# Sliding-window attention into a hard-swish feed-forward: first-tile stores moved to the Pool queue, opening loads, casts and matmuls re-ordered

## The chip, the cores and the metric

The kernel runs on one core of a Trainium2 chip. The metric is device time of one execution in microseconds (us). Eight runs of the kernel before gave a median of 342.49 us (341.08 to 343.52). The profile is one further look at a single execution, the one that took 342.05 us.

## The reference

Inputs are float32: q, k, v of 8 batches x 8 heads x 576 tokens x 64, and two weights, w_in (512 x 2048) and w_out (2048 x 512). The output is 4608 tokens x 512 in float32.

```python
scores = q @ k.T / sqrt(64)
mask = (rel >= 0) & (rel < 64)          # rel = query position - key position
attn = softmax(where(mask, scores, -1e9))
x = (attn @ v), heads side by side      # 4608 tokens x 512
h = x @ w_in
g = h * clip(h + 3, 0, 6) / 6
out = g @ w_out
```

## The kernel before, in words

**The work.** Attention is done batch by batch (576 tokens) and head pair by head pair (four pairs, index `g`). Q and K of a pair are cast to bfloat16 on Pool, transposed (`main_t` for 512 tokens, `rest_t` for the last 64 tokens of all pairs at once), and copied out of PSUM by VectorE and ScalarE. `scores` writes transposed scores, ScalarE takes exp, VectorE multiplies with a band mask (for batch 0 a bias matmul does the masking), `pv` multiplies with V and a column of ones, VectorE normalises, and `xt_pe` transposes the result into `xT`, which holds all of x, transposed. The feed-forward runs over nine tiles of 512 tokens (`T`). `s1(T)` makes 16 blocks (`fc`) of 128 hidden features, four matmuls each over `g`; ScalarE and VectorE turn each into `gT`. `s2(T)` multiplies `gT` with w_out in four blocks of 128 tokens (`ts`), each in four quarters (`u`) of four matmuls; ScalarE copies the block to `osb`, and a DMA stores it.

**The opening.** Batches 0, 1 and 2 are loaded with the SP queue, which carries out its instructions in order: Q and K, the 64-token rests, then V. The weights come as DMAs on the Pool queue that cast to bfloat16 on the way, w_in in four pieces and w_out in four pieces; Pool's casts of Q, K and V stand in the same queue. Three explicit waits (`after`) order the loads: Q and K of batch 1 wait for the second w_in piece, V of batch 1 for the second w_out piece, Q and K of batch 2 for the third. PE does the attention of batch 0, then `s1(0)`, then `s2(0)` mixed with the attention of batch 1 (lines 564 to 597): first two quarters `run(m, 2)`, then transposes and scores of the next pair, three times over. `T_(bt, g)` is the transposes of pair g, `S_` its scores, `N_` its product with V, `X_` the transpose into `xT`; `do` carries out the copy or exp that belongs to an earlier step. From tile 1 on, each tile's matmuls carry the attention of one later batch, and its loads come more than a tile ahead.

**Semaphores of the DMAs.** The framework gives the DMAs of the SP and ACT queues eight completion semaphores in turn (DMAHW0 to DMAHW7), and eight others to those of the Pool queue (DMASW0 to 7). A DMA waits until the earlier one with its semaphore has landed. The four stores of tile 0 stand on the ACT queue (line 422), those of later tiles on SP.

Of the kernel before, what the change touches and what calls it, by code (L numbers as in the profile page):

```python
# [24 lines left out]
def kernel(  # L25
# [73 lines left out]
    def load_qk_for_pe(b, heads):  # L99
        qst = stage.tile([P, H, R * D], F32, name="qst", tag="qst")  # L100
        kst = stage.tile([P, H, R * D], F32, name="kst", tag="kst")
        rst = stage.tile([P, H, D], F32, name="rst", tag="rst")
        ins = []
        for h0 in range(0, H, heads):
            for dst, src in ((qst, q), (kst, k)):
                ins.append(nc.sync.dma_start(  # L106
                    out=dst[:, h0 : h0 + heads, :],
                    in_=src[b, h0 : h0 + heads, 0:SM, :].rearrange("h (p j) d -> p h (j d)", j=R),
                ))
            if h0 == 0:  # L110
                for i, src in enumerate((q, k)):
                    ins.append(nc.sync.dma_start(  # L112
                        out=rst[i * SR : (i + 1) * SR, :, :],
                        in_=src[b, :, SM:S, :].rearrange("h s d -> s h d"),
                    ))
        return (qst, kst, rst), ins

    def load_v_by_head(b):
        vst = stage.tile([P, KB, H, D], F32, name="vst", tag="vst")
        ins = load_blocks(vst, v, b, (KB - 1,)) + load_v(b, vst, 0, H)  # L120
        return vst, ins
# [7 lines left out]
        return tuple(sts), ins  # L129

    ctx.enter_context(tc.manual_schedule())
    stage0, ins0 = load_qk_for_pe(0, 2)
# [29 lines left out]
    QT_ring, KT_ring, P_ring, V_ring = [], [], [], []  # L162
    for i in range(NQT):
        for ring, n in ((QT_ring, "QT"), (KT_ring, "KT")):
            t = consts.tile([P, NG, SP], BF16, name=f"{n}{i}")
            nc.vector.memset(t[:, :, S:SP], 0.0)
            ring.append(t)
    for i in range(NPT):
        t = consts.tile([P, 2, KB, 2 * P], BF16, name=f"pT{i}")
        nc.vector.memset(t[:, :, 0 : KB - 1, QW : 2 * P], 0.0)  # L170
        nc.vector.memset(t[:, :, KB - 1, P : 2 * P], 0.0)
        P_ring.append(t)
    for i in range(NV):
        t = consts.tile([P, KB, H, VW], BF16, name=f"V{i}")
        nc.vector.memset(t[:, :, :, D:VW], 1.0)
        nc.vector.memset(t[D:P, KB - 1, :, 0:D], 0.0)
        V_ring.append(t)
# [5 lines left out]
    xT = consts.tile([P, NG, NT + SP - S], BF16, name="xT")  # L183

    def load_w_in(f0, f1, g0, g1):
        return nc.gpsimd.dma_start(
            out=win16[:, g0:g1, f0:f1],
            in_=moe_w_in[g0 * P : g1 * P, f0:f1].rearrange("(g p) f -> p g f", p=P),
        )
# [179 lines left out]
    def h_tr():  # L369
        return ps_h.tile([P, 1024], BF16, name="hT")  # L370

    def s1_bank(fc):
# [12 lines left out]


    gTs = {}

    def s1(T):
        t0 = T * TB  # L390
        gT = gpool.tile([P, NFC, TB], BF16, name="gT")
        gTs[T] = gT
        for fc in range(NFC):
            hT = s1_bank(fc)
            for g in range(NG):
                nc.tensor.matmul(  # L396
                    hT, lhsT=win16[:, g, fc * P : (fc + 1) * P],
                    rhs=xT[:, g, t0 : t0 + TB], start=(g == 0), stop=(g == NG - 1),
                )
            t1 = t1pool.tile([P, TB], BF16, name="t1")  # L400
            nc.scalar.activation(out=t1[:], in_=hT, func=RELU, bias=half[:], scale=1.0 / 6.0)  # L401
            nc.vector.scalar_tensor_tensor(  # L402
                out=gT[:, fc, :], in0=t1[:], scalar=1.0, in1=hT, op0=MIN, op1=MULT,
            )
            yield

    def s2(T, order):

        gT, accs = gTs[T], {}
        for ts, u in order:  # L410
            if u == 0:
                accs[ts] = next(oa)
            for fc in range(4 * u, 4 * u + 4):
                nc.tensor.matmul(  # L414
                    accs[ts], lhsT=gT[:, fc, ts * P : (ts + 1) * P], rhs=wout16[:, fc, :],
                    start=(fc == 0), stop=(fc == NFC - 1),
                )
            if u == 3:
                osb = osbp.tile([P, DM], F32, name="osb")
                nc.scalar.copy(out=osb[:], in_=accs[ts])  # L420
                u0 = T * TB + ts * P
                (nc.sync if T else nc.scalar).dma_start(out=out[u0 : u0 + P, :], in_=osb[:])
            yield

    BY_BLOCK = [(ts, u) for ts in range(4) for u in range(4)]
# [27 lines left out]
    def do(bt, *key):  # L453
        later.pop((bt.b, *key))()

    def N_(bt, g, banks=None):
        n = [pv(bt, g, h, next(banks) if banks else h_bank()) for h in range(2)]
        n[0]()
        n[1]()

    def X_(bt, g):
        xt_pe(bt, g, h_tr())()

    def TT(bt, g, banks=None):
        T_(bt, g, banks)
        do(bt, "q", g)
        do(bt, "k", g)
# [18 lines left out]
    cast_pairs(bt, st, 0, 2)  # L486
    bt.cast_rest(st, pcopy)
    for g in range(1, NG):
        cast_pairs(bt, st, 2 * g, 2)
    w_in = [load_w_in(0, 512, 0, NG)]  # L490
    bt.cast_v(vst0, KB - 1, KB, 0, H, pcopy)
    bt.cast_v(vst0, 0, KB - 1, 0, 2, pcopy)
    bt.cast_v(vst0, 0, KB - 1, 2, 4, pcopy)
    w_in += [load_w_in(512, 1024, 0, NG)]
    bt.cast_v(vst0, 0, KB - 1, 4, 6, pcopy)
    bt.cast_v(vst0, 0, KB - 1, 6, 8, pcopy)
    w_in += [load_w_in(1024, FF, 0, 2), load_w_in(1024, FF, 2, NG)]
# [9 lines left out]
    later[0, "r"] = bt.rest_t(ps_acc.tile([P, 1024], BF16, name="acc"))  # L507
    do(bt, "q", 0)
    do(bt, "k", 0)
    S0_(0, 0)  # L510
    T0_(1)
    do(bt, "r")
    do(bt, "q", 1)
    do(bt, "s", 0, 0)
    S0_(0, 1)
    do(bt, "k", 1)
    do(bt, "s", 0, 1)
    for g in range(1, NG):
# [10 lines left out]
        do(bt, "s", g, 1)  # L529
    N_(bt, 1, oa)  # L530
# [34 lines left out]
    TT(bt, 0)  # L565
    RR(bt)
    T_(bt, 1)
    S_(bt, 0, 0)
    S_(bt, 0, 1)
# [112 lines left out]
```

## Time and profile before

| | |
|---|---|
| median of 8 runs | 342.49 us (341.08 to 343.52) |
| the profiled execution | 342.05 us, of which its span is 340.2 us |
| PE busy | 313.6 us of the span |
| ScalarE, VectorE, Pool busy | 201.1, 191.7, 82.1 us |
| PE first works on tile 1 | at 77.45 us of the span |

Times in rows of the profile are us from the span's start, and the second number is a duration. PE is TensorE's matmuls, DVE VectorE, ACT ScalarE, POOL GpSimd; SPq and ACTq are the DMA issues of those engines. Text in square brackets is idle time of the engine before the row, and what ended it. L414 is line 414 of the kernel before.

### The profile page before, as it was taken

What the parts mean: (1) busy time and instruction counts of PE and PEld (TensorE: products, weight loads), DVE (VectorE), ACT (ScalarE), POOL (GpSimd) and SP (SyncE); (2) the same over time, 40 slices, a digit from 0 to 9 for tenths busy, and PEclk for the clock granted to TensorE, in tenths of its full rate; (3) what the DMA queues carried; (4) which work ended last, traced back from release to release, by engine and by line L of the source; (5) the groups of instructions that cost most, each with busy time, mean ns of one, the idle gap of its engine ahead of it and who ended that gap; (6) DMA issues with size and microseconds to landing.
All of it is one profiled execution on the core that took longest, in us unless ns stands there. A gap on an engine that the chain in (4) does not pass through costs nothing.

```text
span 340.2 us, 5963 instructions
## 1 busy us (share of the span) xinstructions
PE 313.6 (92%) x2332; PEld 159.6 (47%) x2332; DVE 191.7 (56%) x341; ACT 201.1 (59%) x321; POOL 82.1 (24%) x108
## 2 busy tenths in 40 slices
PE   3969797088999999999999999999999999999995
PEld 1544453054555545644564455445544554444442
DVE  5567643045865476657754786478557646604700
ACT  2757672026885587558746864786478637625811
POOL 5722605520540036203520461038000000000000
PEclk9999899579999999999999999999999999999999
DMA  7999999999307499659976995799400010011011
GB/s 211 223 167 270 171 191 242 246 269 220 81 34 187 127 210 198 165 141 200 194 192 132 209 204 152 149 198 218 134 31 2 31 66 31 3 62 62 2 62 62
DMA packets 128988, 48.89 MB, mean 144 GB/s; under 512 B 114624, under 2 KB 123840, under 8 KB 128960
## 3 DMA queue, kind: packets, MB, share of 16 engines
q1 hardware_dynamic: 124672, 43.27, 59.3%
q0 software_dynamic: 3712, 4.19, 7.8%
q10 hardware_dynamic: 576, 1.05, 0.9%
q8 instruction: 18, 0.29, 0.4%
q14 instruction: 10, 0.08, 0.1%
HBM read 36.70 MB, written 9.44 MB: 136 GB/s over the span
## 4 chain that ended last, share of the span: by engine, by line
PE 78%; DMA 13%; SPq 5%; POOL 1%; ACT 1%; DVE 1%; issue 1%; ACTq 0%; POOLq 0%
PE acc L414 18%; PE o L414 16%; PE hT L396 16%; PE st L396 12%; DMA vst<-in_v_dram 5%; PE st L297 3%; PE hT L332 3%; DMA kst<-in_k_dram 2%; PE hT L358 2%; DMA win<-in_moe_w_in_dram 2%; SPq L106 2%; PE acc L396 2%; PE o L396 2%; PE hT L337 2%; DMA wout<-in_moe_w_out_dram 2%; SPq L112 1%
## 5 line engine op out<-in xcount | busy, mean ns | idle before, releaser
L396 PEld LDWEIGHTS <-win 128*128 128x128 bf16 x576 | 55.5, 98 | 66.2 <-issue 0.7
L414 PEld LDWEIGHTS <-gT 128*128 128x128 bf16 x576 | 53.0, 99 | 68.2 <-issue 13.4
L414 PE MATMUL acc<-wout,gT 128*128 128x512 bf16 x288 | 72.0, 387 | 10.0 <-ACT osb L420 10.0
L402 DVE SCALAR_TENSOR_TENSOR gT<-t,hT 128x512 bf16<-128x512 bf16 x72 | 49.0, 687 | 48.3 <-ACT t L401 48.3
L414 PE MATMUL o<-wout,gT 128*128 128x512 bf16 x288 | 69.6, 383 | 0.1
L396 PE MATMUL hT<-xT,win 128*128 128x512 bf16 x288 | 68.7, 379 | 0.2
L306 ACT ACTIVATE pT<-st 128x768 bf16<-128x768 f32 x64 | 49.2, 809 | 13.5 <-PE st L297 13.4
L401 ACT ACTIVATE t<-hT,half 128x512 bf16<-128x512 f32 x72 | 49.0, 692 | 11.9 <-PE hT L396 11.9
L396 PE MATMUL st<-xT,win 128*128 128x512 bf16 x216 | 51.2, 379 | 0.0
L320 DVE TENSOR_TENSOR pT<-pT,mask 128x1920 bf16<-128x1920 bf16 x28 | 38.5, 1373 | 19.7 <-ACT pT L312 19.7
L401 ACT ACTIVATE t<-st,half 128x512 bf16<-128x512 f32 x54 | 37.1, 688 | 9.4 <-PE st L396 9.1
L402 DVE SCALAR_TENSOR_TENSOR gT<-t,st 128x512 bf16<-128x512 bf16 x54 | 37.2, 688 | 9.1 <-ACT t L401 9.1
L363 ACT COPY xT<-hT 128x576 bf16<-128x576 bf16 x32 | 20.5, 640 | 27.1 <-PE hT L358 26.3
L213 POOL CAST qn<-qst 128x512 bf16<-128x512 f32 x20 | 11.4, 611 | 93.4 <-DMA qst<-in_q_dram 78.0
L208 POOL CAST V<-vst 64x512 bf16<-64x512 f32 (+2 forms) x22 | 26.1, 1203 | 29.7 <-DMA vst<-in_v_dram 26.4
L420 ACT COPY osb<-o 128x512 f32<-128x512 f32 x18 | 10.6, 588 | 34.0 <-PE o L414 33.0
L345 DVE RECIPROCAL rec<-hT 128x5 f32<-128x5 f32 x56 | 10.6, 189 | 35.3 <-PE hT L337 35.3
L348 DVE TENSOR_TENSOR opg<-hT,rec 128x320 bf16<-128x320 f32 x56 | 27.5, 492 | 1.9
L420 ACT COPY osb<-acc 128x512 f32<-128x512 f32 x18 | 10.7, 592 | 28.0 <-PE acc L414 14.4
L332 PEld LDWEIGHTS <-pT 128*128 128x128 bf16 x320 | 21.1, 99 | 10.3 <-issue 2.2
L332 PE MATMUL hT<-V,pT 128*128 128x65 bf16 x280 | 19.6, 195 | 0.9 <-DVE opg L348 0.8
L297 PE MATMUL st<-QT,KT 64*128 64x192 bf16 (+1 forms) x320 | 19.3, 244 | 0.0
(76 smaller groups left out, 236.8 us busy)
## 6 DMA issues: line engine op xcount, KB each, us to landing
out_dram<-osb SPq DMA_DIRECT2D x32, 256.0 KB, 2.0
qst<-in_q_dram SPq DMA_DIRECT2D x24, 256.0 KB, 4.6
kst<-in_k_dram SPq DMA_DIRECT2D x24, 256.0 KB, 5.4
vst<-in_v_dram SPq DMA_DIRECT2D x20, 256.0 KB, 6.0
vst<-in_v_dram SPq DMA_DIRECT2D x32, 128.0 KB, 4.9
win<-in_moe_w_in_dram POOLq DMA_DIRECT2D x4, 512.0 KB, 7.3
qst<-in_q_dram SPq DMA_DIRECT2D x4, 512.0 KB, 7.3
kst<-in_k_dram SPq DMA_DIRECT2D x4, 512.0 KB, 8.1
```

The costliest lines, as they stand in the source:

```text
L208: copy(out=self.V[:kp, k0:k1, h0:h1, 0:D], in_=vst[:kp, k0:k1, h0:h1, :])
L297: nc.tensor.matmul(st[:, h, off : off + w], lhsT=bt.KT[h * D : (h + 1) * D, g, kb * P : (kb + 1) * P], rhs=bt.QT[h * D : (h + 1) * D, g, k ...
L306: nc.scalar.activation(out=pT[:, :, 2 * u : 2 * u + 2, 0:QW], in_=st[:, :, 0 : 2 * QW].rearrange("p h (k w) -> p h k w", k=2), func=EXP, s ...
L320: nc.vector.tensor_tensor(out=pT[:, :, :, 0:QW], in0=pT[:, :, :, 0:QW], in1=mask[:].rearrange("p (h k) w -> p h k w", h=2), op=MULT,)
L332: nc.tensor.matmul(ob, lhsT=pT[:, h, qb, 0:P], rhs=V[:, qb, 2 * g + h, :], start=True, stop=(qb == 0),)
L348: nc.vector.tensor_tensor(out=opgs[bt.b, g][:, :, h, :], in0=ov[:, :, 0:D], in1=rec[:].unsqueeze(2).to_broadcast([P, KB, D]), op=MULT,)
L363: return lambda: acopy(out=xT[:, g, bt.b * S : (bt.b + 1) * S], in_=tr[:, 0:S])
L396: nc.tensor.matmul(hT, lhsT=win16[:, g, fc * P : (fc + 1) * P], rhs=xT[:, g, t0 : t0 + TB], start=(g == 0), stop=(g == NG - 1),)
L401: nc.scalar.activation(out=t1[:], in_=hT, func=RELU, bias=half[:], scale=1.0 / 6.0)
L402: nc.vector.scalar_tensor_tensor(out=gT[:, fc, :], in0=t1[:], scalar=1.0, in1=hT, op0=MIN, op1=MULT,)
L414: nc.tensor.matmul(accs[ts], lhsT=gT[:, fc, ts * P : (ts + 1) * P], rhs=wout16[:, fc, :], start=(fc == 0), stop=(fc == NFC - 1),)
L420: nc.scalar.copy(out=osb[:], in_=accs[ts])
```

## The change

- The four stores of tile 0 are no longer issued at their copies on the ACT queue. They are kept in `held` and issued on the Pool queue, behind the casts of Q and K of batch 2.
- `load_first`: K of head pair 0 of batch 0 goes on the ACT queue, the 64-token rests come after pair 1 and not after pair 0, and V of batch 0 waits until Q of pair 2 has landed.
- Ten dummy matmuls (`keep_busy`) on zeros stand at the start of PE's queue, eight first and two before the first scores. VectorE's memsets are spread between the copies.
- The first w_in piece is issued behind the V cast of pair 0, the other three, now equal pieces, behind the last V cast. Q and K of batch 1 wait for the third piece.
- `s1(0)` begins before the last pair of batch 0 is finished: the first four blocks get their matmuls of pairs 0, 1 and 2 around `X_(bt, 3)`. It uses other PSUM banks.
- w_out pieces are issued among the casts of batch 1: behind Q of heads 0 to 3, behind the rest, and two behind K of heads 4 to 7. The waits of V of batch 1 and of Q and K of batch 2 for w_out pieces are gone.
- The transposes of pair 0 and of the rests of batch 1 move into the end of `s1(0)`.

```diff
+                eng = nc.scalar if h0 == 0 and src is k else nc.sync
...
+    after(insv0[0], ins0[4], "the third pair goes first")
...
+    keep_busy(8)
...
-    def s1(T):
+    def s1(T, first=()):
...
+            for gs in first:
+                for fc in range(4):
+                    mms(fc, banks[fc], gs)
+                yield
...
-                (nc.sync if T else nc.scalar).dma_start(out=out[u0 : u0 + P, :], in_=osb[:])
+                if T:
+                    nc.sync.dma_start(out=out[u0 : u0 + P, :], in_=osb[:])
+                else:
+                    held.append((u0, osb))
...
+    m = s1(0, ((0, 1), (2,)))
+    run(m, 1)
     X_(bt, 3)
+    run(m, 1)
...
-        after(x, w_in[1], "the weights go first")
-    vst1, insv = load_v_by_head(1)
+        after(x, w_in[2], "the weights go first")
+    vst1, _ = load_v_by_head(1)
...
-    run(s1(0))
...
-    cast_pairs(bt, st, 0, 4)
+    bt.cast_qk(st, 0, 0, 4, pcopy)
+    load_w_out(0)
+    bt.cast_qk(st, 1, 0, 4, pcopy)
     bt.cast_rest(st, pcopy)
-    w_out = [load_w_out(0)]
+    load_w_out(1)
     cast_pairs(bt, st, 4, 4)
-    w_out += [load_w_out(i) for i in range(1, 4)]
-    for x in insv:
-        after(x, w_out[1], "the weights go first")
+    load_w_out(2)
+    load_w_out(3)
+    run(m, 15)
+    TT(bt, 0, oa_tr)
+    run(m)
+    RR(bt, oa_tr)
...
-    st2, ins = load_qk_for_pe(2, 4)
-    for x in ins:
-        after(x, w_out[2], "the weights go first")
+    st2, _ = load_qk_for_pe(2, 4)
...
+    for u0, osb in held:
+        nc.gpsimd.dma_start(out=out[u0 : u0 + P, :], in_=osb[:])
```

In the order of the instructions the change shows at three places that the prediction speaks of. The first is ScalarE's queue at the end of tile 0, with the exps of the last pair of batch 1 (`pT`), the copies of the four output blocks (`osb`) and the copies into `xT`; before:

```order
L312 ACTIVATE pT_149<-st_753 128x2x128
L420 COPY osb<-o 128x512 [waits PE_49]
L422 DMA out_dram<-osb 128x512 [waits DMAHW1_49,Activation_49]
L420 COPY osb<-acc 128x512 [waits PE_49]
L422 DMA out_dram<-osb 128x512 [waits DMAHW3_49,Activation_49]
L420 COPY osb<-o 128x512 [waits PE_49]
L422 DMA out_dram<-osb 128x512 [waits DMAHW7_49,Activation_49]
L363 COPY xT<-hT 128x576 [waits PE_49]
L420 COPY osb<-acc 128x512 [waits PE_49]
L422 DMA out_dram<-osb 128x512 [waits DMAHW3_49,Activation_49]
```

and now:

```order
L352 ACTIVATE pT_150<-st_763 128x2x128
L486 COPY osb<-o 128x512 [waits PE_49]
L486 COPY osb<-acc 128x512 [waits PE_49]
L486 COPY osb<-o 128x512 [waits PE_49]
L403 COPY xT<-hT 128x576 [waits PE_49]
L486 COPY osb<-acc 128x512 [waits PE_49]
```

The stores, each of which waits for the semaphore of an earlier load, are gone from between the copies. The second place is Pool's queue from the last V casts of batch 0 to the V casts of batch 1, with the weight pieces (`win`, `wout`) and the casts of batch 1 (`qn`, `kn`, `rn`); before:

```order
L208 CAST V_152<-vst 128x4x2x64 [waits DMAHW2_49,DMAHW1_49]
L186 DMA win_159<-in_moe_w_in_dram 128x2x1024 x2
L233 CAST qn<-qst 128x4x4x64 [waits DMAHW3_49,PE_49,Pool_49]
L233 CAST kn<-kst 128x4x4x64 [waits DMAHW4_49,PE_49,Pool_49]
L240 CAST rn<-rst 128x512 [waits DMAHW6_49,DMAHW5_49]
L192 DMA wout_160<-in_moe_w_out_dram 128x4x512
L233 CAST qn<-qst 128x4x4x64 [waits DMAHW7_49,PE_49,Pool_49]
L233 CAST kn<-kst 128x4x4x64 [waits DMAHW0_49,PE_49,Pool_49]
L192 DMA wout_160<-in_moe_w_out_dram 128x4x512 x3
L208 CAST V_155<-vst 64x8x64 [waits DMAHW1_49]
```

and now:

```order
L248 CAST V_151<-vst 128x4x2x64 [waits DMAHW2_49,DMAHW1_49]
L226 DMA win_158<-in_moe_w_in_dram 128x4x512 x3
L273 CAST qn<-qst 128x4x4x64 [waits DMAHW3_49,PE_49,Pool_49]
L232 DMA wout_159<-in_moe_w_out_dram 128x4x512
L273 CAST kn<-kst 128x4x4x64 [waits DMAHW4_49,PE_49,Pool_49]
L280 CAST rn<-rst 128x512 [waits DMAHW5_49,DMAHW6_49,PE_49,Pool_49]
L232 DMA wout_159<-in_moe_w_out_dram 128x4x512
L273 CAST qn<-qst 128x4x4x64 [waits DMAHW7_49,PE_49,Pool_49]
L273 CAST kn<-kst 128x4x4x64 [waits DMAHW0_49,PE_49,Pool_49]
L232 DMA wout_159<-in_moe_w_out_dram 128x4x512 x2
L248 CAST V_152<-vst 64x8x64 [waits DMAHW1_49]
```

Two w_out pieces, and not one, now stand ahead of the casts of heads 4 to 7, and three w_in pieces behind the last V cast. The third place is SP's queue at the loads of batch 1; before:

```order
L106 DMA qst<-in_q_dram 128x4x256 [waits DMAHW3_49,DMASW1_49,Pool_49]
L106 DMA kst<-in_k_dram 128x4x256 [waits DMAHW4_49,Pool_49]
L112 DMA rst<-in_q_dram 64x8x64 [waits DMAHW5_49]
L112 DMA rst<-in_k_dram 64x8x64 [waits DMAHW6_49]
L106 DMA qst<-in_q_dram 128x4x256 [waits DMAHW7_49]
L106 DMA kst<-in_k_dram 128x4x256 [waits DMAHW0_49]
L93 DMA vst<-in_v_dram 64x8x64 [waits DMAHW1_49,DMAHW2_49,DMASW5_49,Pool_49]
L82 DMA vst<-in_v_dram 128x4x64
```

and now:

```order
L106 DMA qst<-in_q_dram 128x4x256 [waits DMAHW3_49,DMASW2_49,Pool_49]
L106 DMA kst<-in_k_dram 128x4x256 [waits DMAHW4_49,Pool_49]
L112 DMA rst<-in_q_dram 64x8x64 [waits DMAHW5_49]
L112 DMA rst<-in_k_dram 64x8x64 [waits DMAHW6_49]
L106 DMA qst<-in_q_dram 128x4x256 [waits DMAHW7_49]
L106 DMA kst<-in_k_dram 128x4x256 [waits DMAHW0_49]
L93 DMA vst<-in_v_dram 64x8x64 [waits DMAHW2_49,DMAHW1_49,Pool_49]
L82 DMA vst<-in_v_dram 128x4x64
```

The first load of batch 1 waits for the third weight piece (DMASW2), and V of batch 1 waits for no weight piece (DMASW5 is gone).

More of the change, by code (lines that the diff above doesn't have):

```diff
@@ L131, with load_first, keep_busy @@
     ctx.enter_context(tc.manual_schedule())
-    stage0, ins0 = load_qk_for_pe(0, 2)
-    vst0, insv0 = load_v_by_head(0)
+    def load_first():
+        qst = stage.tile([P, H, R * D], F32, name="qst", tag="qst")
+        kst = stage.tile([P, H, R * D], F32, name="kst", tag="kst")
+        rst = stage.tile([P, H, D], F32, name="rst", tag="rst")
+        ins = []
+        for h0 in range(0, H, 2):
+            for dst, src in ((qst, q), (kst, k)):
+                eng = nc.scalar if h0 == 0 and src is k else nc.sync
+                ins.append(eng.dma_start(
+                    out=dst[:, h0 : h0 + 2, :],
+                    in_=src[0, h0 : h0 + 2, 0:SM, :].rearrange("h (p j) d -> p h (j d)", j=R),
+                ))
+            if h0 == 2:
+                for i, src in enumerate((q, k)):
+                    nc.sync.dma_start(
+                        out=rst[i * SR : (i + 1) * SR, :, :],
+                        in_=src[0, :, SM:S, :].rearrange("h s d -> s h d"),
+                    )
+        return (qst, kst, rst), ins
+    stage0, ins0 = load_first()
+    vst0, insv0 = load_v_by_head(0)
+    after(insv0[0], ins0[4], "the third pair goes first")
+    xT = consts.tile([P, NG, NT + SP - S], BF16, name="xT")
+    nc.vector.memset(xT[:, 0, 0:TB], 0.0)
+    idle = ps_o.tile([P, 512], F32, name="o")
+    def keep_busy(n):
+        for _ in range(n):
+            nc.tensor.matmul(
+                idle[:], lhsT=xT[:, 0, 0:P], rhs=xT[:, 0, 0:TB], start=True, stop=True,
+            )
+    keep_busy(8)
     ident = consts.tile([P, P], BF16, name="ident")
@@ L387 @@
     gTs = {}
-    def s1(T):
+    held = []
+    def s1(T, first=()):
         t0 = T * TB
@@ L392, in s1, with mms @@
         gTs[T] = gT
-        for fc in range(NFC):
-            hT = s1_bank(fc)
-            for g in range(NG):
+        def mms(fc, hT, gs):
+            for g in gs:
                 nc.tensor.matmul(
@@ L399, in s1 @@
                 )
+        banks = []
+        if first:
+            for u in range(2):
+                t = ps_st.tile([P, 2, 512], F32, name=f"st{u}")
+                banks += [t[:, 0, :], t[:, 1, :]]
+            for gs in first:
+                for fc in range(4):
+                    mms(fc, banks[fc], gs)
+                yield
+        for fc in range(NFC):
+            if fc < len(banks):
+                hT = banks[fc]
+                if fc % 2 == 0:
+                    mms(fc, hT, (NG - 1,))
+                    mms(fc + 1, banks[fc + 1], (NG - 1,))
+            else:
+                hT = s1_bank(fc, T)
+                mms(fc, hT, range(NG))
             t1 = t1pool.tile([P, TB], BF16, name="t1")
```

64 lines of the change are left out of this document (39 added, 25 removed).

## Prediction

> **What bounds the kernel now.** I read the page first: the busy times, then the chain that ended last.
>
> ```profile
> PE 313.6 (92%) x2332; PEld 159.6 (47%) x2332; DVE 191.7 (56%) x341; ACT 201.1 (59%) x321; POOL 82.1 (24%) x108
> ...
> PE 78%; DMA 13%; SPq 5%; POOL 1%; ACT 1%; DVE 1%; issue 1%; ACTq 0%; POOLq 0%
> ```
>
> PE is the bound for most of the span, but 13% of the chain is DMA. The busy times by stretch say where (columns: stretch and length, then PE, weight loads, DVE, ACT, POOL, the granted PE clock, DMA share, GB/s).
>
> ```profile
> 45.70:66.00 20.30, 11.42 (x92) 5.58 (x87) 6.58 (x10) 6.79 (x12) 8.69 (x11) 0.88 1.14 230
> 66.00:75.00 9.00, 7.63 (x71) 4.36 (x70) 2.56 (x8) 2.40 (x4) 2.44 (x2) 0.70 1.21 273
> 75.00:340.00 265.00, 259.13 (x1874) 130.95 (x1871) 154.93 (x257) 165.60 (x264) 50.29 (x60) 1.00 0.58 122
> ```
>
> From 75 us on PE is busy 259.13 of 265 us at full clock, and DMA has room (0.58). The change leaves that code alone, so its length stays. What can be won lies before tile 1: PE works 11.42 of the 20.30 us from 45.7 on, while DMA is full. The view of waits names the largest hole.
>
> ```profile
> ACT osb L420 <- DMA vst<-in_v_dram: 14.6, 2, 13.6
> ...
> PE acc L414 <- ACT osb L420: 10.0, 1, 10.0
> ...
> PE hT L263 <- POOL qn L233: 4.4, 1, 4.4
> ```
>
> PE (second row) waits once for 10.0 us on a copy of an output block, and ScalarE, which makes it, waits for a load of V, which has nothing to do with that copy. (The third row is PE's wait at the very start.) The timeline shows how that comes about.
>
> ```profile
> 52.43 0.60 ACT L420 COPY osb<-o 128x512 f32<-128x512 f32 x1
> 66.19 0.39 ACTq L422 DMA_DIRECT2D out_dram<-osb  x1
> ...
> 56.22 1.03 PE L414 MATMUL o<-wout,gT 128*128 128x512 bf16 x4
> 67.25 1.87 PE L414 MATMUL acc<-wout,gT 128*128 128x512 bf16 x4 [10.01 <-ACT osb L420]
> 68.91 0.32 PE L332 MATMUL hT<-V,pT 128*128 128x65 bf16 x2
> ...
> 69.92 1.78 PE L414 MATMUL acc<-wout,gT 128*128 128x512 bf16 x4
> ...
> 71.53 0.44 PE L358 MATMUL hT<-ident,opg 128*128 128x128 bf16 x5
> 72.68 0.22 PE L332 MATMUL hT<-V,pT 128*128 128x65 bf16 x2
> 73.22 1.03 PE L414 MATMUL acc<-wout,gT 128*128 128x512 bf16 x4
> 74.09 0.44 PE L358 MATMUL hT<-ident,opg 128*128 128x128 bf16 x5
> ...
> 77.45 2.13 PE L396 MATMUL hT<-xT,win 128*128 128x512 bf16 x8
> ```
>
> The first block was copied at 52.43, but its store, next on ScalarE's queue, could be issued only at 66.19: it waits for the semaphore of an earlier load (DMAHW1, as the order of instructions shows), a V load of batch 2. The next copy stands behind it, its PSUM bank stays full, and PE, which needs that bank, stands still from 57.24 to 67.25. Tile 1 then begins at 77.45.
>
> **The stores.** Without them on its queue ScalarE copies each block when PE has finished it, so the 10.0 us go. The clock goes with them: after the hole, four matmuls take 68.91 - 67.25 = 1.66 and 71.53 - 69.92 = 1.61 us where later they take 74.09 - 73.22 = 0.87, and the product with V takes 69.92 - 68.91 = 1.01 instead of 73.22 - 72.68 = 0.54. That is 0.79 + 0.74 + 0.47 = 2.0 us more. First term: -12.0 us.
>
> The four stores now stand on Pool behind the casts of Q and K of batch 2. Pool waits there for the last copy of tile 0; behind it are V's casts of batch 2. The `osb` buffers are four and tile 1 needs the first again only in its second half.
>
> ```profile
> 64.95 1.04 POOL L233 CAST kn<-kst 128x1024 bf16<-128x1024 f32 x1 [0.80 <-DMA kst<-in_k_dram]
> ...
> 71.13 1.90 POOL L208 CAST V<-vst 128x2048 bf16<-128x2048 f32 x1 [4.58 <-DMA vst<-in_v_dram]
> ...
> 95.37 0.86 PE o L414 x4
> ```
>
> (The last row is from the chain of waits.) Tile 1's second half begins 95.37 - 77.45 = 17.9 us after its start, and the product with V of batch 2, whose cast ends at 73.0 in the old order, comes in it, so not before 84: that cover of 11 us hides a held Pool queue. Q and K of batch 2 are cast by 66.0 already in the old order. The stores cost nothing here; without the cover they would cost their own issue and landing, some 6 to 8 us by the weight pieces below.
>
> **The weights among the casts.** When the hole is gone, the next thing late is the last w_out piece.
>
> ```profile
> 20.86 1.40 POOL L186 DMA_DIRECT2D win<-in_moe_w_in_dram  x2
> ...
> 30.87 1.04 POOL L233 CAST qn<-qst 128x1024 bf16<-128x1024 f32 x1 [8.61 <-DMA qst<-in_q_dram]
> ...
> 33.85 0.62 POOL L240 CAST rn<-rst 128x512 bf16<-128x512 f32 x1 [0.22 <-DMA rst<-in_k_dram]
> ...
> 37.88 1.04 POOL L233 CAST kn<-kst 128x1024 bf16<-128x1024 f32 x1 [0.43 <-DMA kst<-in_k_dram]
> 38.87 2.23 POOL L192 DMA_DIRECT2D wout<-in_moe_w_out_dram  x3
> 51.80 0.61 POOL L208 CAST V<-vst 64x512 bf16<-64x512 f32 x1 [10.70 <-DMA vst<-in_v_dram]
> ...
> 22.74 0.37 SPq L106 DMA_DIRECT2D qst<-in_q_dram  x1
> ...
> 44.35 0.61 SPq L93 DMA_DIRECT2D vst<-in_v_dram  x1
> ...
> 38.87 5.42 DMA wout<-in_moe_w_out_dram
> ...
> L192 POOL DMA_DIRECT2D wout<-in_moe_w_out_dram x4: 742/746/762, 34.4 to 40.3; - x4
> ...
> DMA to landing us min/median/max: 5.4/6.8/10.6
> ...
> 51.10 1.04 PE L414 MATMUL o<-wout,gT 128*128 128x512 bf16 x4
> ...
> 44.00:46.00 2.00, 2.00 (x23) 1.25 (x22) 0.83 (x2) 0.33 (x1) 0.00 (x0) 0.96 1.22 201
> ```
>
> The last w_out piece is issued at 40.3 and lands 10.6 us later, at 50.9; PE's last quarter of the first two blocks starts at 51.10. So without the hole this piece decides, and tile 1 would begin 77.45 - 12.0 - 50.9 = 14.55 us after it.
>
> How do loads fare beside weights? V of batch 1 was issued at 44.35 and cast at 51.80, 7.5 us later, only after the last weight piece had landed; Q of batch 1, issued at 22.74, was cast at 30.87 while w_in pieces ran. I read this as: weights on Pool's queue hold the loads back almost wholly. The Trainium skill (DMA: Bandwidth & Descriptors, section Queues, rings and completion order) says that each DMA engine takes the queues in turn, a packet at a time. By that rule loads and weights would share; these two rows speak against it, and the time by it is the third rival's.
>
> A piece writes 128 x 4 x 512 x 2 bytes = 0.524 MB. At the 201 GB/s of 44 to 46 us, where only weights land, it takes 2.6 us. From 38.87 + 5.42 = 44.3 to 50.9 two pieces land, 3.3 us each. In the new order two pieces are issued before the casts of heads 4 to 7, whose loads they hold back by 2 x 2.6 = 5.2 us (bounds: 0 if nothing is held, 6.6 at 3.3).
>
> Against that, w_in ends a little sooner. Its first piece now comes behind a V cast, so V is less disturbed, and the last V cast comes some 3 us before 20.3 (an estimate: the first piece then starts some 2 us later than at 12.2). Three pieces behind it land 5.4 and then 2.6 to 3.3 apart: 17.5 + 5.4 + 5.2 to 6.6 = 28.1 to 29.5, where the old order has 29.6:
>
> ```profile
> L186 POOL DMA_DIRECT2D win<-in_moe_w_in_dram x4: 698/726/881, 12.2 to 21.6; - x4
> ...
> DMA to landing us min/median/max: 5.5/7.3/8.0
> ```
>
> (21.6 + 8.0.) I take 0.7 us. The cast of K, heads 4 to 7, then ends at 38.9 - 0.7 + 5.2 = 43.4. There the last two w_out pieces are issued: 5.4 us to the first's landing, 3.0 more (between 2.6 and 3.3) to the second's, 51.8. Second term: 51.8 - 50.9 = +0.9 us. V of batch 1 fills the gap in which Pool casts K, so its last part lands sooner than now and holds nobody.
>
> **The rest: no cost, no gain.** K on the ACT queue, the dummy matmuls, the spread memsets, the three head pairs of `s1(0)` and the transposes in it bring PE to `s2(0)` earlier.
>
> ```profile
> 20.98 0.22 PE L332 MATMUL o<-V,pT 128*128 128x65 bf16 x2 [1.39 <-POOL V L208]
> ...
> 35.47 1.89 PE L396 MATMUL hT<-xT,win 128*128 128x512 bf16 x8
> ...
> 41.94 1.89 PE L414 MATMUL o<-wout,gT 128*128 128x512 bf16 x4
> ```
>
> They can win the 1.39 us and most of the 41.94 - 37.36 = 4.6 us between `s1(0)` and `s2(0)`, say 3.0 of them, since transposes and scores stay: 4.4, and 0.86 for the half clock at 41.94 (1.89 against 1.03), 5.3 in all. But PE then comes to the transposes of pair 2 at about 41.94 - 4.4 + 1.7 (eight matmuls) = 39, and waits there for the cast that ends at 43.4 and later for the weights. This is a new wait, and it swallows the gain. If it weren't there, up to 5.3 us would come out. A loss hides there too: the trace shows no dummy matmul, but ten cost at most 10 x 1.87 / 4 = 4.7 us and at least 10 x 1.03 / 4 = 2.6, and the first 4.4 us of PE's queue are a wait for the first cast anyway; what sticks out, below 1 us, is less than the new wait of 4.
>
> **The sum.** 342.05 - 12.0 + 0.9 = 330.95, say 331.0. The profiled execution (span 340.2) is 0.44 below the median of the runs; that is less than the sum is good for. Two medians that differ by less than 0.3%, 1.0 us, count as the same.
>
> **The rivals.** *Rests late* (27%): the rests of batch 1 are cast at 33.85, 2.0 us after Q's cast ends, where the first w_out piece is now issued. If that piece overtakes them, they come only behind its landing at 30.87 + 1.04 - 0.7 + 5.4 = 36.6; with their cast (0.62) the second piece is issued near 37.4, and the loads of heads 4 to 7 pass between the two. Three pieces then follow one another: 37.4 + 5.4 + 5.2 to 6.6 = 48.0 to 49.4, on average 2.2 before 50.9: 342.05 - 12.0 - 2.2 = 327.9. For it: a close race. Against it: the rests were issued ahead.
>
> *PE alone* (6%): the weights come in time, and the front's 5.3 us come out: 342.05 - 12.0 - 5.3 = 324.8. Against it speaks the full DMA share up to 75 us.
>
> *Fair shares* (12%): loads and weights share evenly. The first two pieces then hold K back less, by some 1.5 us, but V of batch 1, no longer held, runs beside the last two and doubles their 5.2 us: 331.0 - 1.5 + 5.2 = 334.7. The rule of turns in the Trainium skill (DMA: Bandwidth & Descriptors, section Queues, rings and completion order) would lead here.
>
> *Slower* (3%): Pool's queue is the new bound. It holds the stores until tile 0's last copy, then V of batch 2, which the stores hold back as weights do. V is wanted at 66.3 + 17.9 = 84.2. To lose the 12 us again and 1 us more, its cast would have to end after 97; the old order has it at 73.0, and four stores at a weight piece's 3 us each make 85: 343 or more only from 6 us a store on.
>
> *The change does not do what it says* (2%): copies still wait for loads, 342.
>
> **How the numbers follow.** The forecast has 50%. Its own range, by the piece at 2.6 to 3.3, is 329.5 to 333. For 8 in 10 I reach down over the second case and up to the fourth: 326.5 to 334.7. Faster by over 0.3% are the forecast and the first three rivals, 95%; the same 2%; slower 3%.
>
> **What would show it.** Right: no wait of PE on `osb`; the matmuls after the first two blocks at 0.87 us per four; K of heads 4 to 7 of batch 1 cast near 43; the last w_out landing near 52; PE waiting some 3 us for that cast and again before the last quarter; tile 1 beginning at 66.3. Wrong: that cast before 41, tile 1 before 64 or after 69, or any wait of more than 2 us after tile 1 has begun.

## The result and the profile after

The changed kernel takes 330.79 us, the median of 11 runs (329.31 to 333.68), beside 342.75 us for the kernel before in the same set; the ratio is 0.9646, 95% interval 0.9621 to 0.9671. The profiled execution took 329.9 us with a span of 327.7 us. Two executions below stand apart and are left out of every median, one of 540 us in the second experiment and the profiled one of the fifth, 1134.59 us, in which TensorE's matmuls took four times as long (eight in 6.88 us).

The page of the kernel after, busy times and the chain that ended last by engine:

```profile
PE 315.5 (96%) x2342; PEld 159.4 (49%) x2342; DVE 192.2 (59%) x342; ACT 199.9 (61%) x321; POOL 84.5 (26%) x112
...
PE 82%; DMA 11%; SPq 3%; POOL 1%; ACT 1%; DVE 0%; issue 0%; POOLq 0%
```

PE works as long as before (315.5 against 313.6 us), in a shorter span. Where the time went is read by cutting both spans at the same two events: the start of the last quarter of the first two output blocks, and the start of tile 1. The kernel before, busy times by stretch:

```profile
0.00:51.10 51.10, 40.75 (x349) 21.38 (x349) 30.97 (x71) 31.18 (x50) 20.68 (x36) 0.97 1.03 205
51.10:77.45 26.35, 14.79 (x136) 8.11 (x133) 7.18 (x18) 5.61 (x10) 11.13 (x12) 0.81 1.16 251
77.45:340.20 262.75, 258.03 (x1855) 130.10 (x1852) 153.56 (x253) 164.32 (x262) 50.29 (x60) 1.00 0.57 121
```

and the kernel after:

```profile
0.00:51.37 51.37, 44.39 (x359) 21.95 (x360) 30.68 (x72) 30.31 (x50) 21.92 (x38) 0.97 1.09 216
51.37:64.95 13.58, 12.70 (x133) 7.38 (x133) 6.96 (x18) 5.30 (x10) 6.74 (x8) 1.00 1.10 236
64.95:327.70 262.75, 258.41 (x1854) 130.03 (x1851) 154.55 (x253) 164.29 (x262) 55.89 (x67) 1.00 0.63 132
```

The third stretch is 262.75 us in both. The second is 12.77 us shorter: PE is busy 12.70 of its 13.58 us, where it had 14.79 of 26.35, and the clock is full instead of 0.81. The first is 0.27 us longer, though most edits of the change lie in it; it varies, and a second profile of the changed kernel, at the end of the experiments, has 52.72 us. The timelines of ScalarE and of PE after show both:

```profile
52.48 0.60 ACT L486 COPY osb<-o 128x512 f32<-128x512 f32 x1
53.29 0.59 ACT L486 COPY osb<-acc 128x512 f32<-128x512 f32 x1 [0.20 <-PE acc L480]
57.34 0.59 ACT L486 COPY osb<-o 128x512 f32<-128x512 f32 x1 [3.46 <-PE o L480]
...
41.40 1.89 PE L480 MATMUL o<-wout,gT 128*128 128x512 bf16 x4 [2.35 <-DMA wout<-in_moe_w_out_dram]
43.08 1.89 PE L480 MATMUL acc<-wout,gT 128*128 128x512 bf16 x4
...
51.37 1.02 PE L480 MATMUL o<-wout,gT 128*128 128x512 bf16 x4
...
58.55 1.03 PE L480 MATMUL acc<-wout,gT 128*128 128x512 bf16 x4
```

The copies (`osb`) now wait for PE, not PE for a copy, so the hole of 10.0 us is gone, and its half clock too. In the opening a new wait stands in the bracket at 41.40: PE comes to the first w_out matmuls 2.35 us before their weights, and then does eight matmuls at half clock (1.89 us for four; later 1.03). The kernel before had no such wait, but half clock at this place too, 1.89 us for the four matmuls at 41.94. Pool's queue and the chain of waits after tell what the weights waited for (the chain's rows have start and length of a piece of the path):

```profile
31.59 1.04 POOL L273 CAST qn<-qst 128x1024 bf16<-128x1024 f32 x1 [11.10 <-PE hT L443]
32.56 0.75 POOL L232 DMA_DIRECT2D wout<-in_moe_w_out_dram  x1
...
35.53 0.62 POOL L280 CAST rn<-rst 128x512 bf16<-128x512 f32 x1 [0.37 <-DMA rst<-in_k_dram]
36.09 0.74 POOL L232 DMA_DIRECT2D wout<-in_moe_w_out_dram  x1
...
38.34 1.04 POOL L273 CAST kn<-kst 128x1024 bf16<-128x1024 f32 x1 [0.46 <-DMA kst<-in_k_dram]
39.33 1.48 POOL L232 DMA_DIRECT2D wout<-in_moe_w_out_dram  x2
...
30.43 7.77 DMA kst<-in_k_dram
...
40.06 11.27 DMA wout<-in_moe_w_out_dram
...
DMA to landing us min/median/max: 8.5/8.7/11.3
```

The first w_out piece is issued at 32.56 and takes 8.5 us or more (the last row, from the view of the tile `wout`; the least was 5.4 before). K of heads 4 to 7 is not held: its cast begins at 38.34. The last piece is issued at 40.06 and lands 11.27 us later, at 51.33; PE's last quarter starts at 51.37.

### The profile page after: what moved, and what is told of

Read it like the earlier page. It is cut to its first block, busy times and chain, and to the rows that moved or that the text cites. A ratio compares the mean times of both kernels' runs of the same rounds, so it can differ in the third digit from the quotient of the medians.

```text
span 327.7 us, 5987 instructions
## 1 busy us (share of the span) xinstructions
PE 315.5 (96%) x2342; PEld 159.4 (49%) x2342; DVE 192.2 (59%) x342; ACT 199.9 (61%) x321; POOL 84.5 (26%) x112
## 3 DMA queue, kind: packets, MB, share of 16 engines
q1 hardware_dynamic: 124400, 43.00, 62.3%
q0 software_dynamic: 4544, 5.24, 9.1%
## 4 chain that ended last, share of the span: by engine, by line
PE 82%; DMA 11%; SPq 3%; POOL 1%; ACT 1%; DVE 0%; issue 0%; POOLq 0%
PE acc L480 19%; PE o L480 18%; PE hT L443 17%; PE st L443 13%; PE st L337 4%; DMA wout<-in_moe_w_out_dram 3%; PE hT L372 3%; PE hT L398 2%; DMA kst<-in_k_dram 2%; DMA win<-in_moe_w_in_dram 2%; PE acc L443 2%; PE o L443 2%; PE hT L377 2%; DMA qst<-in_q_dram 1%; DMA vst<-in_v_dram 1%; SPq L82 1%
## 5 line engine op out<-in xcount | busy, mean ns | idle before, releaser
L468 DVE SCALAR_TENSOR_TENSOR gT<-t,hT 128x512 bf16<-128x512 bf16 x70 | 47.4, 686 | 45.5 <-ACT t L467 45.5
L480 PE MATMUL acc<-wout,gT 128*128 128x512 bf16 x288 | 71.0, 383 | 0.0
L443 PE MATMUL hT<-xT,win 128*128 128x512 bf16 x280 | 66.9, 379 | 0.0
L443 PE MATMUL st<-xT,win 128*128 128x512 bf16 x224 | 53.3, 379 | 1.4 <-DMA win<-in_moe_w_in_dram 1.0
L467 ACT ACTIVATE t<-hT,half 128x512 bf16<-128x512 f32 x70 | 47.4, 693 | 10.6 <-PE hT L443 10.5
L360 DVE TENSOR_TENSOR pT<-pT,mask 128x1920 bf16<-128x1920 bf16 x28 | 39.8, 1423 | 19.1 <-ACT pT L352 19.1
L468 DVE SCALAR_TENSOR_TENSOR gT<-t,st 128x512 bf16<-128x512 bf16 x56 | 38.3, 688 | 12.6 <-ACT t L467 12.5
L467 ACT ACTIVATE t<-st,half 128x512 bf16<-128x512 f32 x56 | 38.3, 688 | 10.8 <-PE st L443 9.0
```

The source lines that it names most:

```text
L360: nc.vector.tensor_tensor(out=pT[:, :, :, 0:QW], in0=pT[:, :, :, 0:QW], in1=mask[:].rearrange("p (h k) w -> p h k w", h=2), op=MULT,)
L443: nc.tensor.matmul(hT, lhsT=win16[:, g, fc * P : (fc + 1) * P], rhs=xT[:, g, t0 : t0 + TB], start=(g == 0), stop=(g == NG - 1),)
L468: nc.vector.scalar_tensor_tensor(out=gT[:, fc, :], in0=t1[:], scalar=1.0, in1=hT, op0=MIN, op1=MULT,)
L480: nc.tensor.matmul(accs[ts], lhsT=gT[:, fc, ts * P : (ts + 1) * P], rhs=wout16[:, fc, :], start=(fc == 0), stop=(fc == NFC - 1),)
```

## The experiments

Two theories were to be told apart. The first term's: the stores on ScalarE's queue are the whole gain. The opening's: the edits at the front are worth something, but the w_out pieces swallow it; then it is open whether the first piece, the half clock or all bytes ahead of the last piece decide. Ratios are to the kernel before, with their 95% intervals.

**The stores alone.** The kernel before with one edit:

```diff
+    held = []
...
-                (nc.sync if T else nc.scalar).dma_start(out=out[u0 : u0 + P, :], in_=osb[:])
+                if T:
+                    nc.sync.dma_start(out=out[u0 : u0 + P, :], in_=osb[:])
+                else:
+                    held.append((u0, osb))
...
+    for u0, osb in held:
+        nc.gpsimd.dma_start(out=out[u0 : u0 + P, :], in_=osb[:])
```

> The kernel before with one part of the change: the four stores of tile 0 go to Pool's queue behind the casts of Q and K of batch 2; all else as before. Theory (the stores are the whole gain; the earlier opening is lost again at w_out): PE's 10 us wait on osb and the half clock behind it are gone, tile 1 begins near 65.2, time 329.5 to 331, the changed kernel's 330.8 within 1 us. Rival (the opening gives part of the gain, the stores less): 333 or more.

Measured: 329.34 us (4 runs), ratio 0.9624 (0.9587 to 0.9661); last quarter at 51.00, tile 1 at 64.53. The stores alone bring the whole gain.

**All but the stores.** The changed kernel with the four stores back at their copies:

```diff
-                if T:
-                    nc.sync.dma_start(out=out[u0 : u0 + P, :], in_=osb[:])
-                else:
-                    held.append((u0, osb))
+                (nc.sync if T else nc.scalar).dma_start(out=out[u0 : u0 + P, :], in_=osb[:])
```

> The changed kernel with one part undone: tile 0's stores stand on ScalarE's queue again, each behind its copy. Theory: each store waits for the semaphore of a V load of batch 2, which lands at 65 to 68 us in the changed kernel; PE stands still from about 57 to 66 and loses some 2 us to the half clock, time 340 to 343. Rival (the new order of loads frees the semaphores earlier, the stores need not move): 334 or less.

Measured: 337.15 us (3 runs), ratio 0.9862 (0.9798 to 0.9926); last quarter at 52.12, tile 1 at 72.32. The hole is back, but smaller than expected (340 to 343 us). Its timelines of ScalarE and PE:

```profile
53.19 0.59 ACT L486 COPY osb<-o 128x512 f32<-128x512 f32 x1
60.08 0.42 ACTq L488 DMA_DIRECT2D out_dram<-osb  x1
60.54 0.59 ACT L486 COPY osb<-acc 128x512 f32<-128x512 f32 x1 [6.77 <-DMA rst<-in_k_dram]
63.72 0.34 ACTq L488 DMA_DIRECT2D out_dram<-osb  x1
...
52.12 1.02 PE L480 MATMUL o<-wout,gT 128*128 128x512 bf16 x4 [0.46 <-DMA wout<-in_moe_w_out_dram]
...
61.17 1.04 PE L480 MATMUL acc<-wout,gT 128*128 128x512 bf16 x4 [3.16 <-ACT osb L486]
63.01 1.90 PE L480 MATMUL acc<-wout,gT 128*128 128x512 bf16 x4
```

In the new order of loads the first store's semaphore belongs to a load that lands earlier: the store is issued at 60.08 and not at 66.19, and ScalarE stands 6.8 us instead of 13.6. So the edits do not add up. The other edits alone gain some 5 us against the kernel before, and gain it at the hole: the stretch from the last quarter to tile 1 takes 20.20 us instead of 26.35, while the one ahead of it is 1.02 us longer. Once the stores are moved there is no hole to shorten.

**Is it the first piece, or the half clock behind it?** One kernel issues every w_out piece one place earlier, the first behind the last w_in piece:

```diff
     w_in += [load_w_in(f, f + 512, 0, NG) for f in (512, 1024, 1536)]
+    load_w_out(0)
...
     bt.cast_qk(st, 0, 0, 4, pcopy)
-    load_w_out(0)
+    load_w_out(1)
     bt.cast_qk(st, 1, 0, 4, pcopy)
     bt.cast_rest(st, pcopy)
-    load_w_out(1)
-    cast_pairs(bt, st, 4, 4)
     load_w_out(2)
+    cast_pairs(bt, st, 4, 4)
     load_w_out(3)
```

> The changed kernel with each w_out piece one place earlier on Pool's queue: the first right behind the last w_in piece, the second behind Q, the third behind the rests, the fourth behind K of batch 1. Theory (tile 0's second half hangs on the landing of the first w_out piece at 41.4, which queues behind the loads of batch 1): the piece lands near 33, PE has no wait before its first w_out matmul and no half clock there, the loads of batch 1 come 2 to 3 us later, tile 1 begins 2 to 3 us sooner, time 327.5 to 329. Rival (all bytes up to the last piece decide, whatever their order): within 1 us of 330.8. Rival of the prediction's step (weights hold the loads back): K of batch 1 is cast after 43 and the time rises above 331.5.

The other has ten matmuls of unused result ahead of the first w_out matmuls, so that the clock holds:

```diff
-    def keep_busy(n):
+    def keep_busy(n, idle=idle):
...
     do(bt, "s", 0, 1)
+    keep_busy(10, ps_acc.tile([P, 512], F32, name="acc"))
     for g in range(1, NG):
```

> The changed kernel with ten more matmuls whose result is not used, put on PE's queue between the first scores of batch 1 and the first w_out matmuls, where PE waits for the first w_out piece. Theory (a gap of 2.4 us and the sparse stretch ahead of it drop the clock, and eight w_out matmuls at half clock cost 1.7 us, with nothing behind them to swallow that): the eight take 0.87 us per four, tile 1 begins 1 to 1.7 us sooner, time 329 to 330. Rival (the later w_out pieces decide, so the loss is swallowed): 330.8 within 0.6. Second rival: the extra matmuls themselves come late, 331.5 or more.

Measured: 329.65 us, ratio 0.9627 (0.9592 to 0.9662), and 330.28 us, 0.9645 (0.9605 to 0.9686); neither differs from the changed kernel. PE's timeline of the second shows why:

```profile
42.42 1.04 PE L480 MATMUL o<-wout,gT 128*128 128x512 bf16 x4 [1.17 <-DMA wout<-in_moe_w_out_dram]
...
45.75 1.02 PE L480 MATMUL o<-wout,gT 128*128 128x512 bf16 x4 [0.49 <-DMA wout<-in_moe_w_out_dram]
...
49.11 1.02 PE L480 MATMUL o<-wout,gT 128*128 128x512 bf16 x3 [0.54 <-DMA wout<-in_moe_w_out_dram]
...
52.91 1.02 PE L480 MATMUL o<-wout,gT 128*128 128x512 bf16 x4 [1.42 <-DMA wout<-in_moe_w_out_dram]
```

The clock holds (1.04 at once), and now PE waits for each later piece; they come 3.3 to 3.8 us apart. The first kernel has no wait and full clock at its first w_out matmuls, at 41.33; its brackets at the three later pieces are 0.73, 0.47 and 1.05 us, its last quarter at 51.63, tile 1 at 65.16. What PE gains at one piece it gives back at the next: neither the first piece nor the clock alone decides.

**V's bytes out of the way.** V of batch 1, which the change lets run beside w_out, waits for the third piece:

```diff
-    vst1, _ = load_v_by_head(1)
+    vst1, insv = load_v_by_head(1)
...
-    load_w_out(2)
+    third = load_w_out(2)
     load_w_out(3)
+    for x in insv:
+        after(x, third, "the weights go first")
```

once in the changed kernel,

> The changed kernel, with the V loads of batch 1 again behind the third w_out piece. Theory A (the bytes ahead of the last piece set the start of tile 1): the pieces land about 2.6 us apart instead of 3.3, the last one near 49.2, the last quarter begins there instead of at 51.37, and the time falls by some 2 us to 328. Theory B (once the first piece is late, TensorE itself, at half clock over its first eight w_out matmuls, fills the time to the last quarter): the first piece lands at 41.3 as before, TensorE needs about 9.9 us from there, and the last quarter stays within 0.4 us of 51.3; the time is that of the changed kernel, 330.8, within 0.5. Rival: V comes so late that TensorE waits for it at the P@V matmuls, and the time grows by over 1 us.

and once with every piece a place earlier as above:

> Every w_out piece one place earlier, as in the third experiment, and the V loads of batch 1 behind the third piece. There the first w_out matmuls began at 41.33 at full clock and TensorE then waited 0.73, 0.47 and 1.05 us for later pieces. Theory A (bytes ahead of the last piece): without V's bytes these waits go, the last quarter begins near 49.4, tile 1 near 62.9, and the time is near 327.5, some 2 us under the changed kernel. Rival: the pieces already had their turn on the rings and V's bytes did not matter; the last quarter stays near 51.6 and the time near 329.7. Second rival: V is waited for later, and what the opening gains is lost there.

Measured: 328.06 us (3 runs), ratio 0.9608 (0.9559 to 0.9657), and 328.99 us, 0.9626 (0.9575 to 0.9678). In the second the waits for the middle pieces are gone and 0.68 us is left before the last quarter, which starts at 50.92 (expected 49.4, and 51.63 with V beside): V's bytes delay the pieces, but the time gains nothing that these runs show (0.9626, and 0.9627 with V beside). For the first, see the repeat below.

**One piece for all quarters.** What is the front worth where w_out is not waited for? Only the first piece is loaded, behind the last w_in piece, and serves all four quarters; the other three loads are left out.

```diff
-                    accs[ts], lhsT=gT[:, fc, ts * P : (ts + 1) * P], rhs=wout16[:, fc, :],
+                    accs[ts], lhsT=gT[:, fc, ts * P : (ts + 1) * P], rhs=wout16[:, fc % 4, :],
...
```

Once with the changed front,

> Only the first w_out piece is loaded, behind the last w_in piece, and all four quarters use it: three loads of 0.5 MB are left out, so part of the product is wrong. TensorE needs about 8.1 us from its first w_out matmul to the last quarter at full clock. Theory (the opening is bound by transfers): no wait for w_out is left, the first w_out matmuls begin at 40 to 41.3, the last quarter at 48.2 to 49.4, tile 1 at 61.7 to 62.9, the time 326 to 327.7. Rival (TensorE or the exps bound the opening anyway): last quarter still near 51, the time 330.

and once with the front of before (the stores moved; the loads that waited for the second or third w_out piece wait for this one):

> The same with the front of the kernel before: the kernel of the first experiment (only the stores moved), with one w_out piece loaded behind the last w_in piece and used for all quarters; three loads are left out here too. It tells what the changed front is worth when w_out is no longer waited for. If the front's edits bring TensorE to the batch-1 scores some 2 us sooner, as the two traces read: first w_out matmuls at 41.8 to 42.5, last quarter at 49.9 to 50.6, the time 328 to 328.8, 1.5 to 2.5 above the seventh experiment. If the front was worth 5.3 us, as the prediction's upper bound had it: 5 us above it. If it is worth nothing: equal to it within 0.5.

Measured: 328.54 us, ratio 0.9611 (0.9572 to 0.965), and 328.38 us, 0.9602 (0.9551 to 0.9653): the same. In the profiled executions the last quarter starts at 49.99 and 50.85; both have four matmuls at half clock, the first of w_in at 37.68 (1.91 us), the second of w_out at 41.96 (1.84 us). The theory of the opening falls with this: with three quarters of w_out's bytes gone the time improves by some 2 us against the changed kernel and 1 us against the stores alone, the intervals overlap, and the changed front is worth nothing beside the old one. PE's timeline with the changed front:

```profile
35.25 0.40 PE L303 MATMUL o<-ident,qn 128*128 128x128 bf16 x4 [0.99 <-POOL qn L273]
37.38 0.50 PE L303 MATMUL acc<-ident,kn 128*128 128x128 bf16 x4 [1.73 <-POOL kn L273]
37.68 1.91 PE L443 MATMUL hT<-xT,win 128*128 128x512 bf16 x4
...
41.89 1.04 PE L480 MATMUL o<-wout,gT 128*128 128x512 bf16 x4
...
49.99 1.04 PE L480 MATMUL o<-wout,gT 128*128 128x512 bf16 x4
```

PE now waits a step earlier, for the casts of Q and K of batch 1 (0.99 and 1.73 us), whose loads still come behind w_in. From 41.89 it runs without a wait, and needs 8.1 us to the last quarter.

**Side by side.** The changed kernel, the stores alone, V behind the third piece, and V behind the third piece with the ten dummy matmuls, unchanged from above or put together from it, on one chip:

> The changed kernel itself, once more, beside the three others on the same chip. Theory (the whole gain is the stores', and the front's edits are worth nothing in the end): equal to the kernel with the stores alone within 0.3%. Rival (the front's edits cost something, as the first call's 329.3 against 330.8 would have it): 0.3 to 0.5% slower than that kernel.

> The kernel before with only the stores of tile 0 moved, as in the first experiment. Theory: equal to the changed kernel within 0.3%, ratio to the kernel before 0.963 to 0.965. Rival: 1 to 1.5 us under the changed kernel.

> The changed kernel with the V loads of batch 1 behind the third w_out piece, as in the fifth experiment, whose profiled execution was no use. Theory A (bytes ahead of the last piece): pieces 2.6 us apart, last quarter near 49.2, tile 1 near 62.8, some 2 us under the changed kernel. Theory B (TensorE at half clock fills the time from the first piece on): half clock over the first eight w_out matmuls as before, no wait for a later piece, last quarter within 0.5 of 51.3, time within 0.3% of the changed kernel.

> The same with ten matmuls of unused result between the first scores of batch 1 and the first w_out matmuls, as in the fourth experiment, so that the clock holds while the first piece is waited for. If bytes and half clock both held the opening, each hiding the other, now both are gone: first w_out matmuls near 41.5 to 42.4 at full clock, no wait or under 0.5 us for later pieces, last quarter at 49.6 to 50.5, tile 1 at 63.2 to 64.0, time 0.9 to 1.7 us under the changed kernel. Rival: the pieces stay as they were in the fourth experiment (waits of 0.5, 0.5 and 1.4 us), and the time equals the changed kernel's.

| kernel | median us | ratio | 95% interval | last quarter | tile 1 |
|---|---|---|---|---|---|
| changed kernel | 330.68 | 0.9648 | 0.9616 to 0.968 | 52.72 | 66.25 |
| stores alone | 329.47 | 0.9606 | 0.9572 to 0.9639 | 50.23 | 63.77 |
| V behind the third piece | 328.28 | 0.9582 | 0.955 to 0.9615 | 51.44 | 65.23 |
| the same with dummies | 327.81 | 0.9575 | 0.9541 to 0.9609 | 49.86 | 63.39 |

The last two columns are from the one profiled execution of each kernel (330.75, 328.15, 329.86 and 327.90 us).

The stores alone come out 1.2 us under the changed kernel. The intervals still overlap, but of the five runs of each only one pair does (329.83 against 329.80), so it is likely, not settled, that the other edits cost something; that they bring nothing is plain. The two kernels with V held back beat the changed kernel (their intervals lie just below its own), the last by 2.9 us or 0.9% (expected 0.9 to 1.7 us); against the stores alone, which keep V behind the second piece as the kernel before does, nothing is settled. So of the other edits the one that took V's wait away is one that costs, in the changed order of the pieces; with every piece a place earlier, above, holding V back gained no time. Whether it acts by theory A or B stays open: the third kernel's profile caught the slowest of its six runs, 329.86 us, with half clock and no wait for a later piece, as theory B has it; its median of 328.28 is what theory A gave, and no profile shows such an execution. The granted clock of the whole execution is 0.988 in the profiled run and 0.995 to 1.0 in the five faster ones, so part of the difference goes with the clock. With the dummies, both causes gone, the last quarter starts at 49.86, as expected. PE's timeline of the changed kernel in this set:

```profile
42.68 1.89 PE L480 MATMUL o<-wout,gT 128*128 128x512 bf16 x4 [3.27 <-DMA wout<-in_moe_w_out_dram]
44.36 1.79 PE L480 MATMUL acc<-wout,gT 128*128 128x512 bf16 x4
...
52.72 1.02 PE L480 MATMUL o<-wout,gT 128*128 128x512 bf16 x4 [0.30 <-DMA wout<-in_moe_w_out_dram]
```

and that of the last kernel, with the landing times of its pieces:

```profile
41.30 1.03 PE L480 MATMUL o<-wout,gT 128*128 128x512 bf16 x4
42.17 1.03 PE L480 MATMUL acc<-wout,gT 128*128 128x512 bf16 x4
...
49.86 1.02 PE L480 MATMUL o<-wout,gT 128*128 128x512 bf16 x4 [0.41 <-DMA wout<-in_moe_w_out_dram]
...
DMA to landing us min/median/max: 6.8/7.4/9.4
```

With V beside them the pieces of the fourth experiment took 8.7, 9.5 and 11.8 us (least, median, most); that kernel differs from the last one in V's wait alone. So with V beside them each piece lands some 2 us later after its issue; that counts the time behind the pieces ahead of it. The wait of 3.27 us and the half clock of the first rows are gone here.

## Why the prediction was right, and where it was not

The forecast was 331.0 us, and the median is 330.79.

**First term: right.** It was -12.0 us; the stretch from the last quarter to tile 1 shrank by 12.77. The hole and the half clock behind it are gone as the timelines show, and the first two experiments show that the stores were their cause. PE's timeline after, at the places where the prediction reads the kernel before (56.22, 67.25, 74.09 and 77.45), gives the parts:

```profile
56.28 1.03 PE L480 MATMUL o<-wout,gT 128*128 128x512 bf16 x4
57.14 1.03 PE L480 MATMUL acc<-wout,gT 128*128 128x512 bf16 x4
...
61.96 0.44 PE L398 MATMUL hT<-ident,opg 128*128 128x128 bf16 x5
...
64.95 2.07 PE L443 MATMUL hT<-xT,win 128*128 128x512 bf16 x8
```

The hole is worth 11.03 - 0.86 = 10.17 us (56.22 to 67.25, 56.28 to 57.14) and the half clock behind it 6.84 - 4.82 = 2.02 (67.25 to 74.09, 57.14 to 61.96), together 12.19. Of the 0.58 us more, 0.21 lies ahead of the hole and 0.37 in the tail behind the half clock (3.36 and 2.99 us), which the term left out; no run measured these by themselves.

**Second term: the number came out, its mechanism did not.** It was +0.9 us; measured +0.27 (51.10 to 51.37), and +1.62 in the second profile (52.72). That it lies near the forecast is luck. The step that failed is "weights on Pool's queue hold the loads back almost wholly". By it K of heads 4 to 7 would be cast by 43.4; it was cast by 39.4, and a cast before 41 stood in the text as a sign of error. The load of K had been issued at 30.43, ahead of the first w_out piece at 32.56, and landed at 38.20; by the trace's records of packets the piece moved its first one at 36.38. A piece that is issued behind queued loads is the one that is late: the first w_out piece took 8.5 us or more, not 5.4. So the last piece was issued 3.3 us sooner than forecast and took 11.27 us instead of the 8.4 that the working gave it (5.4 and 3.0): two errors that nearly cancel, 51.33 against 51.8. From there on loads and weights share the DMA engines. How they share fits the page of the kernel after:

```profile
q1 hardware_dynamic: 124400, 43.00, 62.3%
q0 software_dynamic: 4544, 5.24, 9.1%
```

Packets and MB of SP's queue and of Pool's, over the whole span: 43.00 MB / 124400 = 346 bytes a packet and 5.24 / 4544 = 1153 bytes. If the queues take turns by packet, weights get 1153 / (1153 + 346) = 77% of the bytes, and a piece of 2.6 us alone takes 2.6 / 0.77 = 3.4 us beside V; the fourth experiment shows 3.3 to 3.8. The records of packets show the turns themselves: from 42 to 50 us Pool's queue moved 1221 packets of 1024 bytes and SP's 1228 of 256 bytes, 156 and 39 GB/s, so the weights got 80%. The Trainium skill (DMA: Bandwidth & Descriptors, section Queues, rings and completion order) states such turns, and these records agree with it. The failed step rested on V of the kernel before, and for that load it was right: by the same records V was issued at 44.35 behind two queued pieces and moved nothing until 48.4, while the weights moved at 177 GB/s. Why it had no turn in these 4 us stays open. The error was to carry the hold over to loads that are issued ahead of the pieces.

**The rest: swallowed, though not by the wait that was named.** PE did not wait 3 to 4 us for the cast of K. In the profiled execution it waited 2.35 us for the first w_out piece and lost 1.7 us at half clock behind it. The upper bound of 5.3 us behind that wait was not to be had: with one w_out piece instead of four the old and the new front take the same time, and in the new one PE then waits for Q and K of batch 1. That the loads of the opening as a whole, not one piece, set its length is argued from these waits; no run made those loads shorter.

**The rivals.** *Rests late* did not occur (cast at 35.53). *PE alone*, 324.8, was not reached even with three pieces left out. *Fair shares* was right that V runs beside the pieces, but shared the bytes evenly and put 5.2 us on V's, where the packets' sizes make it some 0.8 us a piece (3.4 against 2.6); giving V back its place was worth 2.4 us, not 5.2. *Slower*: Pool's queue held nobody, the stores' cover was as reckoned, and from tile 1 on both spans are 262.75 us. The copies no longer wait for loads, so the change does what it says.

## What to carry to other kernels

A store on a queue of a compute engine can be held by the completion semaphore of a load that has nothing to do with it; the wait then shows up as the engine's idle time "<- DMA" of an unrelated tile. Here it stood 13.6 us and was worth the whole gain, while the rest of the opening's tuning brought nothing. When an engine waits for a transfer, ask which transfers were issued ahead of it, and hold back those that are needed later. Take two changes apart before adding their gains: here the second lived off the hole that the first one closed.

## What the runs showed of the hardware

A pause much shorter than the hole of before was enough to halve the clock. The busy times by stretch of the changed kernel (the granted clock stands third from the right):

```profile
38.00:40.00 2.00, 0.94 (x16) 0.58 (x13) 0.91 (x3) 1.51 (x3) 1.66 (x2) 1.00 1.21 203
40.00:42.00 2.00, 0.60 (x2) 0.28 (x3) 0.00 (x0) 1.14 (x3) 1.24 (x3) 0.85 1.26 233
42.00:44.00 2.00, 2.00 (x7) 0.65 (x5) 0.00 (x0) 0.00 (x0) 0.19 (x1) 0.50 1.21 195
44.00:46.00 2.00, 2.00 (x22) 1.15 (x21) 0.77 (x2) 0.27 (x1) 0.00 (x0) 0.80 1.22 196
```

PE stood still for 2.35 us only, but was busy for no more than 1.54 of 4 us around it. The Trainium skill (TensorE: Matmul & The Clock Gate, section Why this matters for your kernels) warns of idle gaps over about 3 us; here a shorter one did it, and with V held back the clock was at half behind a wait of 1.61 us as well. The kernel before needed no such wait: PE's longest one between 36 and 42 us was 0.64 us, and the clock fell all the same. With the stores alone it held, in both profiles of that kernel. From 40 to 42 us, the kernel before first, then the first experiment:

```profile
40.00:42.00 2.00, 1.67 (x19) 1.08 (x19) 0.86 (x2) 0.75 (x2) 1.10 (x2) 0.68 0.62 94
40.00:42.00 2.00, 1.59 (x23) 1.00 (x21) 0.98 (x2) 0.91 (x3) 1.54 (x3) 1.00 0.67 101
```

In both PE is busy 4.26 of the 6 us from 36 on, and the first four w_out matmuls take 1.89 us in the one (at 41.94) and 1.04 in the other (at 41.76). So the same opening comes out with half clock and without it, and a difference of 1 us between two single profiles should not be put down to an edit.
